# Output projection of eight tiles in four pairs by seven products of halves

## Chip, cores and metric

The kernel runs on one core of a Trainium2 chip. The metric is the device time of one execution in microseconds.

## Reference

Layer norm, sliding attention with dilation (32 heads of 20, window of 8 positions two apart), output projection, and a gate from a bilinear feed-forward layer.

```python
B, S, D, F = 1, 2048, 640, 1536
xn = layernorm(x)                              # no scale, no shift
q, k, v = heads(xn @ wqkv)                     # 32 heads of 20
logits = q . k[pos - 2 * (0..7)] * 20 ** -0.5  # positions below 0 masked
o = softmax(logits) @ v[pos - 2 * (0..7)]
s = o @ wo                                     # (2048, 640) @ (640, 640): the part changed
h = (xn @ w_gate) * (xn @ w_up)                # (2048, 1536)
out = x + s * silu(h @ w_down)
```

All is float32. A product is made of three: each operand is split into a high part (fp32r) and a low part, and high x high, high x low and low x high are summed (`mm3`, `ALL3`).

## The kernel before

The 2048 positions are 16 tiles of 128. The order on each engine is the order of the source; buffers are taken by tag (`st(shape, tag, bufs)`), and an operation waits until the buffer it takes is free. PSUM tags are q (4 banks), g (2) and u (2).

The stages follow each other and overlap. Norm and transposition of the tiles come first; then twelve units (`qkv`, `attention`) of q, k, v, whose attention runs on VectorE while TensorE works on pieces of gate and up (`gate_up(f, ch)`: block f of 12, 512 positions ch of 4). The last two blocks are f0 = 10 and f1 = 11; their eight pieces are written out by hand. In a piece, the first half of the matmuls fills a g bank, ScalarE copies it (`gs`, L409), the second half fills a u bank, and VectorE multiplies the two into `hs` (L420). This multiplication is issued a piece later (`finish_piece`), behind what the source puts on VectorE's queue between the pieces; the very last is made by ScalarE (L422) and GpSimd (L423). hs goes to `h_scr` in DRAM.

Then comes the output projection. `load_o` fetches attention rows of up to three tiles from `o_scr`, `trans_o` transposes a tile on VectorE (L481) and splits it (`split`, L85 on ScalarE for the high part, L86 for the low part), and `out_proj` makes two halves of 320 columns of 15 matmuls each: 5 blocks of the contraction x 3 parts. ScalarE copies each (L498); `s_scr` holds the results. The weights wo are loaded by `load_wo` and split by `split_wo` on ScalarE and GpSimd, five blocks k. Beside it, in twelve steps, the weights of the down projection are loaded (`load_wd`), summed on VectorE (`sum_wd`, L529 to L535) and split on ScalarE and GpSimd (`split_wd`).

Last, the down projection: pairs of tiles by seven products of halves in the Strassen-Winograd form (`product`, L620; `gather`; sums of h in `sum_h`, high and low parts in `hi_h`, `lo_h`), with silu, the gate and the result.

All DMAs are issued by the SP queue, in order. `load_h` fetches the pieces of h.

Of the kernel before, what the change touches and what calls it, by code (L numbers as in the profile page):

```python
# [11 lines left out]
F32 = mybir.dt.float32  # L12
F32R = mybir.dt.float32r
AF = mybir.ActivationFunctionType
# [5 lines left out]
P = 128  # L20
S, D, F = 2048, 640, 1536
# [16 lines left out]
SCALE = DH ** -0.5  # L38
MASKED = -1e9 / SCALE
EPS = 1e-5  # L40
PAIRS = range(0, W, 2)
PACE = 1.0

# [7 lines left out]
def kernel(  # L51
# [23 lines left out]
    def st(shape, tag, bufs, dt=F32):  # L75
        cnt[0] += 1
        return sb.tile(shape, dt, tag=tag, bufs=bufs, name=f"{tag}_{cnt[0]}")

    def pt(shape, tag, bufs):
        cnt[0] += 1  # L80
        return ps.tile(shape, F32, tag=tag, bufs=bufs, name=f"{tag}_{cnt[0]}")

    def split(eng, raw, hi, lo):

        nc.scalar.activation(hi, raw, AF.Copy)  # L85
        eng.tensor_sub(lo, raw, hi.bitcast(F32))  # L86
# [3 lines left out]
    def mm3(acc, pairs, parts=ALL3, first=True, last=True):  # L90

        pairs = list(pairs)
        runs = [(a[i], b[j]) for i, j in parts for a, b in pairs]
        for n, (a, b) in enumerate(runs):
            nc.tensor.matmul(acc, a, b, start=first and n == 0, stop=last and n == len(runs) - 1)  # L95
# [356 lines left out]
    def load_wo(ks):  # L452
        t = st([P, 2, D], "wraw", 3)
        for n, k in enumerate(ks):
            nc.sync.dma_start(t[:, n, :], wo[:, k, :])
            wo_raw[k] = t[:, n, :]
        return t

    def split_wo(k):
        if k < KD - 1:  # L460
            y = st([P, 2, D], ("wf", "wf", "wqh", "wql")[k], (4, 4, 1, 1)[k], F32R)
            hi, lo = y[:, 0], y[:, 1]
        else:
# [6 lines left out]
    def load_o(s, n, t):  # L470


        for b in range(NQ):
            nc.sync.dma_start(t[b * QB:(b + 1) * QB].rearrange("i n (q c) -> i (n q) c", c=QC),
                              o_scr[s // NE, b, s % NE:s % NE + n].rearrange("n (q i) c -> i (n q) c", i=QB))
        for i in range(n):
            o_t[s + i] = t[:, i]

    def trans_o(s):
        y = st([P, KD, P], "ot", 2)  # L480
        nc.vector.transpose(y.rearrange("p k (q i) -> p k q i", i=QB),  # L481
                            o_t.pop(s).rearrange("p (q k j) -> p k q j", q=NQ, j=QB))
        if s == NT - 2:
            oT[s] = st([P, KD, P], "hs", 2, F32R), st([P, KD, P], "hs", 2, F32R)
        else:
            tag, n = ("kv", 2) if s == 0 else ("wf", 4) if s < NT - 2 else ("t", 2)
            z = st([P, 2, KD, P], tag, n, F32R)
            oT[s] = z[:, 0], z[:, 1]
        split(nc.vector, y, *oT[s])

    def out_proj(s):
        a = oT.pop(s)
        y = st([P, D], "hs" if s % 2 and s < NT - 4 else "gs", 2)
        for n in range(2):
            c = slice(n * HALF, (n + 1) * HALF)
            p = pt([P, HALF], "q", 4)
            mm3(p, [([t[:, k, :] for t in a], [t[:, c] for t in wo_s[k]]) for k in range(KD)])
            nc.scalar.activation(y[:, c], p, AF.Copy)  # L498
        nc.sync.dma_start(s_scr[s], y)


    KH = KF // 2
# [1 line left out]
    W_IN = ("B11", "T1", "T2", "B22", "T3", "B21", "T4")  # L504
    H_IN = ("A11", "S1", "S2", "S4", "S3", "A12", "A22")

    def begin_wd():

        big = [st([P, KH + 2, 2, HALF], "xc", NCH, F32R) for _ in range(4)]
        for name, y in zip(("B11", "T1", "T2", "B21"), big):  # L510
            wd_t[name] = [y[:, k] for k in range(KH)]
        wd_t["T3"] = [big[k // 2][:, KH + k % 2] for k in range(KH)]
        for name in ("B22", "T4"):
            y = st([P, KH, 2, HALF], "kv", 2, F32R)
            wd_t[name] = [y[:, k] for k in range(KH)]

    def load_wd(k):
        wd_raw[k] = st([P, 2, 2, HALF], "wraw", 3)
        for a in range(2):
            nc.sync.dma_start(wd_raw[k][:, a].rearrange("p a c -> p (a c)"), wd[:, a * KH + k, :])  # L520
# [16 lines left out]
    def split_wd(k, part):  # L537
        for name in (("B11", "B22", "T1"), ("B21", "T2", "T3", "T4"))[part]:
            split(nc.gpsimd, wd_v[k][name], *(wd_t[name][k][:, i] for i in range(2)))
        if part:  # L540
            wd_raw.pop(k), wd_v.pop(k)

    h_raw, hT = {}, {}

    def load_h(n):

        a, b = 2 * n, 2 * n + 1
        if n % 2:
            ta, tb = st([P, KF, P], "t", 2), st([P, KF, P], "t", 2)
            nc.sync.dma_start(ta, h_scr[a])  # L550
            nc.sync.dma_start(tb, h_scr[b])
            h_raw[n] = {"A11": ta[:, :KH], "A12": ta[:, KH:], "A21": tb[:, :KH], "A22": tb[:, KH:]}
        else:
            h_raw[n] = {}
            for name, s, k, tag, m in (("A11", a, 0, "wraw", 3), ("A21", b, 0, "wraw", 3),
                                       ("A22", b, KH, "wraw", 3), ("A12", a, KH, "o", 1)):
                h_raw[n][name] = st([P, KH, P], tag, m)
                nc.sync.dma_start(h_raw[n][name], h_scr[s][:, k:k + KH])

# [63 lines left out]
    def gather(m):  # L623

        n, j = divmod(m, 7)
        a, b = 2 * n, 2 * n + 1
        p = bank["ACACABA"[j]]
        if j == 0:
            keep("M1", p, "lg", 2)
        elif j == 1:  # L630
            keep("M5", p, "lg", 2)
        elif j == 2:
            keep("U2", p, "e", 1)
        elif j == 3:
# [12 lines left out]
        return lambda: None  # L647


    begin_unit(0)  # L650
# [121 lines left out]
    for u in range(2, len(UN)):  # L772
        unit(u)
        for _ in range(3 + (u in (2, 5)) if u + 1 < len(UN) else len(pieces)):
            if len(pieces) == 1:
                load_wf(f1)
            piece()
    for ch in range(NCH):
        gate_up(f0, ch)
        if ch == 0:  # L780
            split_wf(f1, nc.gpsimd)
            load_wo((0, 1))
            load_wo((2, 3))
            t = load_wo((4,))
    for ch in range(NCH):
        if ch == 3:
            load_wd(0)
            trans_o(0)
            load_o(1, 1, st([P, 1, D], "o", 1))
            load_o(2, 3, st([P, 3, D], "t", 2))  # L790
            load_o(5, 3, st([P, 3, D], "t", 2))
        gate_up(f1, ch)
        if ch < 3:
            for k in ((0, 1), (2, 3), (4,))[ch]:
                split_wo(k)
        if ch == 1:
            drain(len(UN) - 2)
            load_o(0, 1, t[:, 1:2])
        if ch == 2:
            advance(1e9)  # L800

    load_wd(1)
    o_next = {3: (8, 3), 6: (11, 3), 9: (14, 2)}
    n_prod = 7 * NT // 2
    for s in range(NT):
        k, part = divmod(s - 1, 2)
        if s == 1:
            begin_wd()
        if s + 1 < NT:
            trans_o(s + 1)  # L810
        if s in o_next:
            load_o(*o_next[s], st([P, o_next[s][1], D], "t", 2))
        if 0 <= k < KH:
            sum_wd(k, part)
        out_proj(s)
        if 0 <= k < KH:
            split_wd(k, part)
            if part and k + 2 < KH:
                load_wd(k + 2)
        if s == 12:  # L820
            load_h(0)
        if s == 14:
            hi_h(0)
            lo_h(0)
# [72 lines left out]
```

## Time and profile before

| | |
|---|---|
| median of 3 runs | 782.94 us (782.87 to 783.04) |
| profiled execution | 783.04 us |
| its span, first to last instruction | 781.3 us |
| TensorE busy | 774.8 us, 4432 matmuls |
| VectorE busy | 670.1 us |
| ScalarE busy | 231.1 us |
| GpSimd busy | 135.8 us |

The span is what the profile shows of an execution; the rest of its time lies around it. Times of rows count from the span's start. PE is TensorE, PEld its weight loads, DVE VectorE, ACT ScalarE, POOL GpSimd, SPq the queue of the DMAs. L86 is line 86 of the kernel. `out<-in` names the program's tiles by tag; an idle time stands in brackets with what ended it.

### The profile page before, as it was taken

The numbers are of one execution on the slowest core, as the hardware profiler recorded it, in microseconds if no ns is written. First come the engines' busy times: TensorE is split into PE (matmuls) and PEld (weight loads), VectorE is DVE, ScalarE is ACT, GpSimd is POOL, SyncE is SP. The second block draws the span as 40 slices with busy tenths as digits, with TensorE's granted clock in tenths as the row PEclk, the third lists the DMA queues.
The fourth block names the chain that finished last, engine by engine and source line by source line (L and its number), as shares of the span: only waits on it lengthen the run. The fifth ranks groups of instructions, "written<-read, shape, count | busy, mean of one in ns | idle before, by whom it ended". The sixth has DMA issues, their size and how long they took to land.

```text
span 781.3 us, 11212 instructions
## 1 busy us (share of the span) xinstructions
PE 774.8 (99%) x4432; PEld 706.4 (90%) x4432; DVE 670.1 (86%) x694; ACT 231.1 (30%) x527; POOL 135.8 (17%) x109
## 2 busy tenths in 40 slices
PE   8999999999999999999999999999999999999997
PEld 7989898898988898989898989888899999999997
DVE  7999898999999999996999999995368677777775
ACT  4323312031112121312131212112256554444442
POOL 5200401021013101210204001023177600000000
PEclk9999999999999999999999999999999999999999
DMA  9562131331224122423133131432967574555534
GB/s 320 174 195 75 43 96 38 96 90 48 85 50 124 49 64 81 119 61 79 29 100 91 39 105 39 128 101 70 242 186 216 167 264 156 200 191 182 182 102 136
DMA packets 82237, 93.99 MB, mean 120 GB/s; under 512 B 23096, under 2 KB 63368, under 8 KB 82056
## 3 DMA queue, kind: packets, MB, share of 16 engines
q1 hardware_dynamic: 82184, 93.27, 39.2%
q8 instruction: 35, 0.57, 0.3%
q14 instruction: 18, 0.15, 0.1%
HBM read 55.84 MB, written 28.31 MB: 108 GB/s over the span
## 4 chain that ended last, share of the span: by engine, by line
PE 98%; DMA 0%; ACT 0%; SPq 0%; DVE 0%; issue 0%
PE q L306 27%; PE u L95 22%; PE g L95 22%; PE q L620 11%; PE q L95 9%; PE u L620 5%; PE g L620 3%; DMA wraw<-in_wqkv 0%; SPq L135 0%; ACT xc L231 0%; ACT wqh L85 0%; PE q L230 0%; DVE q L606 0%; DVE q L607 0%; ACT q L601 0%
## 5 line engine op out<-in xcount | busy, mean ns | idle before, releaser
L95 PE MATMUL u<-xc,wf 128*128 128x512 f32 (+1 forms) x735 | 176.2, 390 | 0.0
L95 PE MATMUL g<-xc,wf 128*128 128x512 f32 (+1 forms) x735 | 176.2, 390 | 0.0
L95 PEld LDWEIGHTS u<-xc,wf 128*128 128x128 f32 x735 | 135.7, 187 | 32.1
L95 PEld LDWEIGHTS g<-xc,wf 128*128 128x128 f32 x735 | 135.3, 188 | 31.0
L306 PE MATMUL q<-wqh,xc 128*128 128x300 f32 (+1 forms) x960 | 160.5, 310 | 0.3 <-ACT xc L231 0.2
L306 PEld LDWEIGHTS q<-wqh,xc 128*128 128x128 f32 x960 | 146.3, 188 | 2.7 <-ACT xc L231 0.8
L340 DVE TENSOR_TENSOR t<-q,kv 128x1600 f32<-128x1600 f32 (+1 forms) x48 | 96.9, 2019 | 8.2 <-ACT gs L409 7.2
L361 DVE TENSOR_TENSOR t<-e,kv 128x1600 f32<-128x1600 f32 (+1 forms) x48 | 97.6, 2049 | 1.1
L86 POOL TENSOR_TENSOR wf<-wraw,wf 128x256 fp32r<-128x256 f32 (+2 forms) x22 | 47.8, 2190 | 281.2 <-ACT wf L85 281.2
L343 DVE TENSOR_REDUCE lg<-t 128x80 f32<-128x1600 f32 (+1 forms) x48 | 92.6, 1929 | 1.1
L409 ACT ACTIVATE gs<-g 128x512 f32<-128x512 f32 x48 | 28.7, 598 | 213.8 <-PE g L95 208.6
L306 PE MATMUL q<-wql,xc 128*128 128x300 f32 (+1 forms) x480 | 86.2, 309 | 0.0
L369 DVE TENSOR_TENSOR t<-t,t 128x1600 f32<-128x1600 f32 (+1 forms) x36 | 75.2, 2089 | 1.0
L308 ACT ACTIVATE kv<-q 128x200 f32<-128x200 f32 (+1 forms) x96 | 33.4, 348 | 143.3 <-PE q L306 143.1
L306 PEld LDWEIGHTS q<-wql,xc 128*128 128x128 f32 x480 | 74.8, 188 | 0.0
L620 PE MATMUL q<-xc,wf 128*128 128x320 f32 x432 | 67.2, 308 | 0.0
L620 PEld LDWEIGHTS q<-xc,wf 128*128 128x128 f32 x432 | 64.3, 188 | 0.0
L86 POOL TENSOR_TENSOR wql<-wraw,wqh 128x300 fp32r<-128x300 f32 (+4 forms) x14 | 33.2, 2394 | 168.1 <-ACT wqh L85 168.0
L420 DVE TENSOR_TENSOR hs<-u,gs 128x512 f32<-128x512 f32 x47 | 32.1, 682 | 10.4 <-PE u L95 9.5
L95 PE MATMUL q<-wf,wf 128*128 128x320 f32 x156 | 35.1, 305 | 0.0
L86 DVE TENSOR_TENSOR wf<-ot,wf 128x640 fp32r<-128x640 f32 x13 | 15.0, 1157 | 21.0 <-ACT wf L85 18.1
L95 PEld LDWEIGHTS q<-wf,wf 128*128 128x128 f32 x156 | 26.0, 188 | 0.0
(172 smaller groups left out, 883.4 us busy)
## 6 DMA issues: line engine op xcount, KB each, us to landing
h_scr<-hs SPq DMA_DIRECT2D x48, 256.0 KB, 2.4
wraw<-in_wgu SPq DMA_DIRECT2D x12, 640.0 KB, 4.7
t<-h_scr SPq DMA_DIRECT2D x8, 768.0 KB, 7.7
hs<-s_scr SPq DMA_DIRECT2D x16, 320.0 KB, 3.6
gs<-in_x SPq DMA_DIRECT2D x16, 320.0 KB, 4.2
wraw<-h_scr SPq DMA_DIRECT2D x12, 384.0 KB, 6.3
out<-q SPq DMA_DIRECT2D x14, 320.0 KB, 2.6
wraw<-in_wd SPq DMA_DIRECT2D x12, 320.0 KB, 3.9
```

Of the source, the lines that this page charges most:

```text
L86: eng.tensor_sub(lo, raw, hi.bitcast(F32))
L95: nc.tensor.matmul(acc, a, b, start=first and n == 0, stop=last and n == len(runs) - 1)
L306: nc.tensor.matmul(p, xT[(r * NE + i) // TPC][a][:, k, t0:t0 + P], wq[g][b][:, k], start=n == 0, stop=n == len(runs) - 1, skip_group_check ...
L308: nc.scalar.activation(kv_t[u][:, :, W - 1 + i, :], p[:, c:].rearrange("p (a c) -> p a c", a=2), AF.Copy)
L340: nc.vector.tensor_mul(t, q.rearrange("p i c -> p (i c)").unsqueeze(1).to_broadcast([P, 2, NE * c]), places(0, j))
L343: nc.vector.tensor_reduce(out=lg[:, :, j:j + 2].rearrange("p n a -> p a n"), in_=heads(t), op=ALU.add, axis=AX.X)
L361: nc.vector.tensor_mul(heads(t), pw, heads(places(1, j)))
L369: nc.vector.tensor_add(acc, acc, t)
L409: nc.scalar.activation(gs, pp[0], AF.Copy)
L420: nc.vector.tensor_mul(hs, pp[1], gs)
L620: nc.tensor.matmul(p, y[:, i, k], wd_t[name][k][:, l], start=new and r == 0, stop=r == len(runs) - 1, skip_group_check=True)
```

## The change

Tiles 0 to 7 are projected as four pairs. The pair's rows are a 2 x 2 matrix of blocks (two tiles by two halves of two contraction blocks each), wo's first four blocks are another (two by two halves of 320 columns), and seven products of halves give the four results, in the order and banks of the down projection. The fifth contraction block is added directly: three matmuls in each of products 3 to 6, in product 6 with the difference of its two column halves. The sums of wo (`sums_wo`, `sum_w5`) are made in place in its raw buffers and split by ScalarE and GpSimd (`split_t`, `split_w5`); the sums of a pair are made by VectorE (`turn_pair`), the high parts by ScalarE (`hi_pair`), the low parts by VectorE (`lo_pair`). These operands lie in pieces of buffers that the down projection's weights take later (`blocks`). Pair 0 is loaded after piece (f0, 2) into the buffer of k and v that is free by then.

Blocks 2 and 3 of wo are split after pieces (f0, 1) and (f0, 2) instead of after (f1, 1); the sums and splits of wo and the first pairs stand between the pieces of f1. The twelve steps of the down weights run to tile 14 instead of tile 12, two of them together in pair 3. `load_h(0)` is issued in two parts, and A21 goes to another buffer. Tiles 8 to 15 are projected as before.

```diff
-    def trans_o(s):
-        y = st([P, KD, P], "ot", 2)
+    def turn(y, s):
         nc.vector.transpose(y.rearrange("p k (q i) -> p k q i", i=QB),
                             o_t.pop(s).rearrange("p (q k j) -> p k q j", q=NQ, j=QB))
...
+    def blocks(y, r, h, n):
+        return y[:, r:].rearrange("p r i c -> p (r i c)")[:, :h * n * P].rearrange("p (h n c) -> p h n c", h=h, c=P)
...
+    def sums_wo():
+        r, u = wo_keep
+        b11, b12, b21, b22 = r[:, :, :HALF], r[:, :, HALF:], u[:, :, :HALF], u[:, :, HALF:]
+        nc.vector.tensor_sub(b11, b12, b11)
+        nc.vector.tensor_sub(b12, b22, b12)
+        nc.vector.tensor_sub(b22, b22, b11)
+        nc.vector.tensor_sub(b21, b21, b22)
+        wo_keep.append({"T1": b11, "T3": b12, "T2": b22, "T4": b21})
+
+    def sum_w5():
+        w = wo_keep[3]
+        nc.vector.tensor_sub(w[:, :HALF], w[:, :HALF], w[:, HALF:])
+
+    def split_t(name, y, r):
+        v = wo_keep[2][name]
+        t = y[:, r:r + KS]
+        split(nc.gpsimd, v, t[:, :, 0], t[:, :, 1])
...
+    def turn_pair(p):
+        y = pair_y[p] = st([P, 2, KD, P], "ot", 2)
+        for i in range(2):
+            turn(y[:, i], 2 * p + i)
+        s1, s2, s4 = (pair_raw[p][:, i * KS:(i + 1) * KS] for i in range(3))
+        a11, a12, a21, a22 = (y[:, i, k:k + KS] for i in range(2) for k in (0, KS))
+        nc.vector.tensor_add(s1, a21, a22)
+        nc.vector.tensor_sub(s2, s1, a11)
+        nc.vector.tensor_sub(s4, a12, s2)
+        nc.vector.tensor_sub(a21, a11, a21)
...
+    def hi_pair(p, part):
...
+        nc.scalar.activation(z[0], raw, AF.Copy)
+
+    def lo_pair(p, part):
+        z, raw = pair_z[p, part]
+        nc.vector.tensor_sub(z[1], raw, z[0].bitcast(F32))
...
+    FIFTH = {3: ("a5", HALF), 4: ("b5", HALF), 5: ("a5", 0), 6: ("b5", None)}
+
+    def pair_product(p, j):
+        place = "ACACABA"[j]
+        new = j in (0, 1, 5)
...
+        runs = [(pair_in(p, H_IN[j], k, i), w_part(W_IN[j], k, l)) for i, l in ALL3 for k in range(KS)]
+        if j in FIFTH:
+            name, c = FIFTH[j]
+            runs += [(pair_in(p, name, 0, i), wo_t["W0-W1"][:, l] if c is None else wo_s[KD - 1][l][:, c:c + HALF])
+                     for i, l in ALL3]
+        for r, (y, w) in enumerate(runs):
+            nc.tensor.matmul(b, y, w, start=new and r == 0, stop=r == len(runs) - 1, skip_group_check=True)
+        kept, (ya, yb) = pair_k[0], y_t.setdefault((p, "y"), [None, None])
+        if j < 3:
+            nc.scalar.activation(kept[:, j], b, AF.Copy)
...
     for ch in range(NCH):
         gate_up(f0, ch)
         if ch == 0:
             split_wf(f1, nc.gpsimd)
...
+        elif ch < 3:
+            split_wo(ch + 1)
+        if ch == 2:
             drain(len(UN) - 2)
+            load_pair(0)
+    gate_up(f1, 0)
+    advance(1e9)
+    split_wo(0)
+    split_wo(1)
+    load_pair(1)
+    load_pair(2)
+    begin_wd("T4")
+    begin_wd()
+    turn_pair(0)
+    gate_up(f1, 1)
+    split_wo(4)
+    for i in range(3):
+        hi_pair(0, i)
+    sums_wo()
+    wo_keep.append(w5)
+    split_t("T1", wd_big[0], 4)
+    split_t("T2", wd_big[0], 6)
+    sum_w5()
+    split_w5()
+    for i in range(3):
+        lo_pair(0, i)
+    begin_wd()
+    turn_pair(1)
+    gate_up(f1, 2)
+    split_t("T3", wd_big[1], 4)
+    split_t("T4", wd_big[1], 6)
+    load_wd(0)
     load_wd(1)
+    begin_wd()
+    turn_pair(2)
+    gate_up(f1, 3)
+    begin_wd()
+    begin_wd("B22")
+    sum_wd(0, 0)
...
+    pair_product(0, 0)
+    for p in range(SP // 2):
+        more = p + 1 < SP // 2
+        n = (1, 0, 1, 2)[p]
+        if not more:
+            y8 = turn_o(SP)
+        wd_sums(n)
+        pair_product(p, 1)
+        if more:
+            hi_pair(p + 1, 0)
+            lo_pair(p + 1, 0)
+        else:
+            split_o(SP, y8)
+        pair_product(p, 2)
+        if more:
+            hi_pair(p + 1, 2)
+        pair_product(p, 3)
+        if more:
+            lo_pair(p + 1, 2)
+            hi_pair(p + 1, 1)
+        if p == 0:
+            split_wd(0, 0)
+        pair_product(p, 4)
+        wd_splits(n)
+        if more:
+            lo_pair(p + 1, 1)
+        pair_product(p, 5)
+        if p == 0:
+            load_pair(3)
+        elif p == 1:
+            load_o(SP, 3, st([P, 3, D], "t", 2))
+            turn_pair(3)
+        elif p == 2:
+            load_o(SP + 3, 3, st([P, 3, D], "t", 2))
+        if more:
+            pair_product(p + 1, 0)
+        else:
+            out_proj(SP, 0)
+        pair_product(p, 6)
...
+            load_h(0, ("A11", "A21", "A12"))
+        elif s == 13:
+            load_h(0, ("A22",))
```

More of the change, by code (lines that the diff above doesn't have):

```diff
@@ L40 @@
 EPS = 1e-5
+SP = NT // 2
 PAIRS = range(0, W, 2)
@@ L477, in load_o, with turn_o, trans_o, split_o @@
             o_t[s + i] = t[:, i]
-    def trans_o(s):
-        y = st([P, KD, P], "ot", 2)
+    def turn(y, s):
         nc.vector.transpose(y.rearrange("p k (q i) -> p k q i", i=QB),
                             o_t.pop(s).rearrange("p (q k j) -> p k q j", q=NQ, j=QB))
+    one_t = []
+    def turn_o(s):
+        if not one_t:
+            one_t.append(st([P, 2, KD, P], "ot", 2))
+        y = one_t[0][:, s % 2]
+        turn(y, s)
+        return y
+    def trans_o(s):
+        split_o(s, turn_o(s))
+    def split_o(s, y):
         if s == NT - 2:
@@ L485, in trans_o, with out_proj @@
         else:
-            tag, n = ("kv", 2) if s == 0 else ("wf", 4) if s < NT - 2 else ("t", 2)
-            z = st([P, 2, KD, P], tag, n, F32R)
+            if s == SP:
+                z = blocks(wd_kv["B22"], 4, 2, KD)
+            else:
+                z = st([P, 2, KD, P], *(("wf", 4) if s < NT - 2 else ("t", 2)), F32R)
             oT[s] = z[:, 0], z[:, 1]
         split(nc.vector, y, *oT[s])
[L491 to L499, printed above, removed]
+    y_t = {}
+    def out_proj(s, n):
+        a = oT[s]
+        if n == 0:
+            y_t[s] = st([P, D], "hs" if s % 2 and s < NT - 4 else "gs", 2)
+        c = slice(n * HALF, (n + 1) * HALF)
+        p = pt([P, HALF], "q", 4)
+        mm3(p, [([t[:, k, :] for t in a], [t[:, c] for t in wo_s[k]]) for k in range(KD)])
+        nc.scalar.activation(y_t[s][:, c], p, AF.Copy)
+        if n:
+            oT.pop(s)
+            nc.sync.dma_start(s_scr[s], y_t.pop(s))
     KH = KF // 2
@@ L505, with begin_wd @@
     H_IN = ("A11", "S1", "S2", "S4", "S3", "A12", "A22")
[L507 to L515, printed above, removed]
+    wd_big, wd_kv = [], {}
+    def begin_wd(kv=None):
+        if kv:
+            y = wd_kv[kv] = st([P, KH, 2, HALF], "kv", 2, F32R)
+            wd_t[kv] = [y[:, k] for k in range(KH)]
+            return
+        y = st([P, KH + 2, 2, HALF], "xc", NCH, F32R)
+        wd_t[("B11", "T1", "T2", "B21")[len(wd_big)]] = [y[:, k] for k in range(KH)]
+        wd_big.append(y)
+        if len(wd_big) == NCH:
+            wd_t["T3"] = [wd_big[b][:, k] for b, k in ((2, 6), (2, 7), (3, 7), (3, 6), (1, 6), (1, 7))]
+    def blocks(y, r, h, n):
+        return y[:, r:].rearrange("p r i c -> p (r i c)")[:, :h * n * P].rearrange("p (h n c) -> p h n c", h=h, c=P)
     def load_wd(k):
@@ L543, with load_h @@
     h_raw, hT = {}, {}
-    def load_h(n):
+    def load_h(n, names=()):
         a, b = 2 * n, 2 * n + 1
@@ L553, in load_h @@
         else:
-            h_raw[n] = {}
-            for name, s, k, tag, m in (("A11", a, 0, "wraw", 3), ("A21", b, 0, "wraw", 3),
-                                       ("A22", b, KH, "wraw", 3), ("A12", a, KH, "o", 1)):
+            h_raw.setdefault(n, {})
+            for name, s, k, tag, m in (("A11", a, 0, "wraw", 3), ("A21", b, 0, *(("wraw", 3) if n else ("ot", 2))),
+                                       ("A12", a, KH, "o", 1), ("A22", b, KH, "wraw", 3)):
+                if names and name not in names:
+                    continue
                 h_raw[n][name] = st([P, KH, P], tag, m)
@@ L647, in gather @@
         return lambda: None
+    KS = KD // 2
+    wo_t = {}
+    def sums_wo():
[9 more added lines that the diff above has]
+        nc.vector.tensor_sub(w[:, :HALF], w[:, :HALF], w[:, HALF:])
@@ new lines, in split_t, with split_w5, w_part @@
+    def split_t(name, y, r):
+        v = wo_keep[2][name]
+        t = y[:, r:r + KS]
+        split(nc.gpsimd, v, t[:, :, 0], t[:, :, 1])
+        wo_t[name] = [t[:, k] for k in range(KS)]
+    def split_w5():
+        t = wd_kv["T4"][:, KH - 1]
+        split(nc.gpsimd, wo_keep[3][:, :HALF], t[:, 0], t[:, 1])
+        wo_t["W0-W1"] = t
+    def w_part(name, k, l):
+        if name in wo_t:
+            return wo_t[name][k][:, l]
+        a, c = divmod(int(name[1:]) - 11, 10)
+        return wo_s[a * KS + k][l][:, c * HALF:(c + 1) * HALF]
@@ new lines, with load_pair @@
+    pair_raw, pair_y, pair_z, pair_k = {}, {}, {}, []
+    def load_pair(p):
+        if p:
+            t = st([P, 3, D], "t", 2)
+            load_o(2 * p, 2, t[:, 0:2])
+            t = t.rearrange("p a c -> p (a c)")
+        else:
+            t = st([P, 2, D], "kv", 2)
+            load_o(0, 2, t)
+            t = t.rearrange("p a c -> p (a c)")
+        pair_raw[p] = t[:, :3 * KS * P].rearrange("p (a c) -> p a c", c=P)
+    def turn_pair(p):
[8 more added lines that the diff above has]
+        nc.vector.tensor_sub(a21, a11, a21)
@@ new lines, in hi_pair @@
+    def hi_pair(p, part):
+        if part == 2:
+            if p % 2:
+                z = [st([P, 2, KD, P], "wf", 4, F32R).rearrange("p a k c -> p (a k) c")[:, :3 * KS] for _ in range(2)]
+            else:
+                z = blocks(wd_kv["T4"], 2, 2, 3 * KS) if p else blocks(wd_big[0], 1, 2, 3 * KS)
+                z = [z[:, 0], z[:, 1]]
+            raw = pair_raw[p]
+        else:
+            y, r = (wd_big[3], 3) if p % 2 else (wd_kv["B22"], 2) if p else (wd_kv["T4"], 1)
+            z = blocks(y, r, 2, 2 * KD)
+            z = [z[:, i, part * KD:(part + 1) * KD] for i in range(2)]
+            raw = pair_y[p][:, part]
+        pair_z[p, part] = z, raw
+        nc.scalar.activation(z[0], raw, AF.Copy)
@@ new lines, in lo_pair, with pair_in @@
+    def lo_pair(p, part):
+        z, raw = pair_z[p, part]
+        nc.vector.tensor_sub(z[1], raw, z[0].bitcast(F32))
+    def pair_in(p, name, k, i):
+        part, b = {"A11": (0, 0), "A12": (0, KS), "a5": (0, 2 * KS), "S3": (1, 0), "A22": (1, KS), "b5": (1, 2 * KS),
+                   "S1": (2, 0), "S2": (2, KS), "S4": (2, 2 * KS)}[name]
+        return pair_z[p, part][0][i][:, b + k]
+    FIFTH = {3: ("a5", HALF), 4: ("b5", HALF), 5: ("a5", 0), 6: ("b5", None)}
+    def pair_product(p, j):
+        place = "ACACABA"[j]
+        new = j in (0, 1, 5)
+        if new:
+            bank[p, place] = pt([P, HALF], {"A": "q", "B": "g", "C": "u"}[place], {"A": 4, "B": 2, "C": 2}[place])
+        b = bank[p, place]
+        runs = [(pair_in(p, H_IN[j], k, i), w_part(W_IN[j], k, l)) for i, l in ALL3 for k in range(KS)]
[8 more added lines that the diff above has]
+            nc.scalar.activation(kept[:, j], b, AF.Copy)
+        elif j == 3:
+            ya = y_t[p, "y"][0] = st([P, D], "gs", 2)
+            nc.vector.tensor_add(ya[:, HALF:], kept[:, 2], b)
+        elif j == 4:
+            yb = y_t[p, "y"][1] = st([P, D], "hs", 2)
+            nc.vector.tensor_add(yb[:, HALF:], kept[:, 1], b)
+        elif j == 5:
+            nc.vector.tensor_add(ya[:, :HALF], kept[:, 0], b)
+            nc.sync.dma_start(s_scr[2 * p], ya)
+        else:
+            nc.scalar.activation(yb[:, :HALF], b, AF.Copy)
+            nc.sync.dma_start(s_scr[2 * p + 1], yb)
@@ L777 @@
             piece()
+    wo_keep = []
     for ch in range(NCH):
@@ L781, with wd_sums, wd_splits @@
             split_wf(f1, nc.gpsimd)
[L782 to L796, printed above, removed]
-            drain(len(UN) - 2)
-            load_o(0, 1, t[:, 1:2])
-        if ch == 2:
-            advance(1e9)
-    load_wd(1)
[L803 to L813, printed above, removed]
+            wo_keep += [load_wo((0, 1)), load_wo((2, 3))]
+            w5 = load_wo((4,))[:, 0]
+        elif ch < 3:
+            split_wo(ch + 1)
+        if ch == 2:
+            drain(len(UN) - 2)
+            load_pair(0)
[26 more added lines that the diff above has]
+    load_wd(0)
+    load_wd(1)
+    begin_wd()
[4 more added lines that the diff above has]
+    sum_wd(0, 0)
+    pair_k.append(st([P, 3, HALF], "o", 1))
+    wd_steps = [(k, part) for k in range(KH) for part in range(2)][1:]
+    def wd_sums(n):
+        for k, part in wd_steps[:n]:
             sum_wd(k, part)
-        out_proj(s)
-        if 0 <= k < KH:
+    def wd_splits(n):
+        for k, part in wd_steps[:n]:
             split_wd(k, part)
@@ L819 @@
                 load_wd(k + 2)
+        del wd_steps[:n]
+    pair_product(0, 0)
[9 more added lines that the diff above has]
+            lo_pair(p + 1, 0)
+        else:
+            split_o(SP, y8)
[22 more added lines that the diff above has]
+            pair_product(p + 1, 0)
+        else:
+            out_proj(SP, 0)
+        pair_product(p, 6)
+    n_prod = 7 * NT // 2
+    for s in range(SP, NT):
+        if s + 1 < NT:
+            trans_o(s + 1)
+        if s == SP + 2:
+            load_o(SP + 6, 2, st([P, 2, D], "t", 2))
+        wd_sums(1)
+        if s > SP:
+            out_proj(s, 0)
+        out_proj(s, 1)
+        wd_splits(1)
         if s == 12:
-            load_h(0)
+            load_h(0, ("A11", "A21", "A12"))
+        elif s == 13:
+            load_h(0, ("A22",))
         if s == 14:
```

## The prediction

> **What bounds the kernel now.** I read the parts of the page first: busy time, the chain that ended last, then TensorE's list of waits.
>
> ```profile
> span 781.3 us, 11212 instructions
> PE 774.8 (99%) x4432; PEld 706.4 (90%) x4432; DVE 670.1 (86%) x694; ACT 231.1 (30%) x527; POOL 135.8 (17%) x109
> PE 98%; DMA 0%; ACT 0%; SPq 0%; DVE 0%; issue 0%
> PE q L157 <- POOL ident masks.py:199: 1.4, 1, 1.4
> PE q L230 <- issue: 0.3, 1, 0.3
> PE q L306 <- ACT xc L231: 0.2, 1, 0.2
> ```
>
> The first two lines are the span and the busy times, the third the chain by engine, the last three TensorE's whole list of waits (total, times, longest): 1.9 us, all at the start. TensorE's stream is the time. A matmul taken out counts in full, and so does every wait put in, unless another engine's cover holds. So I price the matmuls, then look for the engine whose cover is thin. A difference under 0.2% (1.6 us: 781.4 to 784.5 about the median 782.94) is about what a measurement here can't tell from none.
>
> **The matmuls.** The pitch of the projection comes from ScalarE's copies of its results (start, us, what): the first half tile and the last, 31 halves apart. The pitch of products by halves comes from the windows view of the down projection (stretch, its us, PE busy and count, PEld, DVE, ACT, POOL).
>
> ```profile
> 561.50 0.44 ACT L498 ACTIVATE gs<-q 128x320 f32<-128x320 f32 x1 [1.03 <-PE q L95]
> 629.14 0.44 ACT L498 ACTIVATE gs<-q 128x320 f32<-128x320 f32 x1 [1.74 <-PE q L95]
> 629.00:781.00 152.00, 147.90 (x1009) 147.64 (x1007) 115.71 (x147) 67.81 (x113) 0.00 (x0) 1.00 0.51 179
> ```
>
> 67.64 / 31 = 2.182 us for 15 matmuls, 0.1455 each. A pair of tiles costs 60 now. After, it costs 7 products x 2 blocks x 3 parts = 42, and the fifth block of the contraction adds 3 to each of four products: 54. Eight tiles: 240 x 0.1455 = 34.9 us become 216. In the down projection a matmul of the same 320 columns takes 147.90 / 1008 = 0.1467 us; at this pitch 216 take 31.7, at the other 31.4. The gain is **3.2 to 3.5 us**. I take 3.2, since the second row's form is the one the change uses.
>
> **What VectorE and GpSimd get to do while gate and up still run.** Their covers decide, so here is that stretch (start, us, engine, line, what, idle before).
>
> ```profile
> 534.14 1.16 DVE L372 TENSOR_TENSOR o<-t 128x960 f32<-128x960 f32 x1
> 538.30 0.69 DVE L420 TENSOR_TENSOR hs<-u,gs 128x512 f32<-128x512 f32 x1 [3.00 <-PE u L95]
> 545.30 0.69 DVE L420 TENSOR_TENSOR hs<-u,gs 128x512 f32<-128x512 f32 x1 [6.31 <-PE u L95]
> 545.90 0.83 DVE L481 STREAM_TRANSPOSE ot<-wraw 128x640 f32<-128x640 f32 x1
> 550.63 1.67 DVE L86 TENSOR_TENSOR kv<-ot,kv 128x640 fp32r<-128x640 f32 x1 [3.89 <-ACT kv L85]
> 552.24 0.69 DVE L420 TENSOR_TENSOR hs<-u,gs 128x512 f32<-128x512 f32 x1
> 536.04 3.09 POOL L86 TENSOR_TENSOR wf<-wraw,wf 128x640 fp32r<-128x640 f32 x2 [22.92 <-ACT wf L85]
> 544.56 1.58 POOL L86 TENSOR_TENSOR wql<-wraw,wql 128x640 fp32r<-128x640 f32 x1
> 550.04 1.57 POOL L86 TENSOR_TENSOR q<-wraw,q 128x640 fp32r<-128x640 f32 x1 [3.90 <-ACT q L85]
> ```
>
> The attention ends at 535.3. A piece of gate and up takes 7.0 us (538.30 to 545.30). VectorE multiplies each piece's u out of its bank (L420) as soon as the piece ends, and idles between.
>
> Two operations with both inputs in SBUF exclude each other: at 550.63 VectorE's subtraction takes 1.67 us beside GpSimd's that began at 550.04, and ends 0.69 after it. Alone the same form takes 0.83:
>
> ```profile
> 580.46 0.83 DVE L86 TENSOR_TENSOR wf<-ot,wf 128x640 fp32r<-128x640 f32 x1 [0.87 <-ACT wf L85]
> 581.20 0.48 DVE L534 TENSOR_TENSOR wraw<-wraw 128x320 f32<-128x320 f32 x1
> 583.71 1.50 DVE L86 TENSOR_TENSOR wf<-ot,wf 128x640 fp32r<-128x640 f32 x1 [0.87 <-ACT wf L85]
> 585.13 1.16 DVE L529 TENSOR_TENSOR lg<-wraw 128x320 f32<-128x320 f32 x1
> 584.49 1.46 POOL L86 TENSOR_TENSOR kv<-e,kv 128x320 fp32r<-128x320 f32 x1
> ```
>
> GpSimd's 584.49 waits in turn for VectorE's end at 585.21, and L529 for GpSimd's end at 585.95: they take turns. The multiplication out of a bank (0.69 at 545.30, under GpSimd's 544.56) and the transposition (0.83 at 545.90) aren't delayed. The Trainium skill ("SBUF — State Buffer", Who interferes with whom) says the same and speaks against this change: GpSimd shares a port pair with VectorE as an exclusive lock, and a tensor_tensor with both inputs in SBUF contends. Were that not so, only the sum without lock, below, would hold.
>
> Into this stretch the change puts, in VectorE's order: two transpositions and four sums of 256 columns (turn_pair 0), the multiplication of piece (f1, 0), four sums of 640 (sums_wo), one of 320, three low parts (640, 640, 768), turn_pair(1), and only then the multiplication of piece (f1, 1). By start-to-start times (0.74 for 640 at 580.46; 0.41 for 320; by the same slope 0.34 for 256 and 0.87 for 768; 0.1 more where an operation reads the one before), a turn_pair is 3.25, sums_wo 3.2, the low parts 2.4, with sum_w5 0.4 and two multiplications 1.3: 13.8 us. **Without lock**, from 535.3, that ends at 549.1. On GpSimd stand eight splits: blocks 0, 1, 4, then T1, T2, W0-W1, T3, T4, 1.5 us each, one 0.8.
>
> When must it be done? The u banks are two: piece (f1, 3) writes (f1, 1)'s, from the middle of the piece on.
>
> ```profile
> 516.48 0.56 DVE L356 TENSOR_TENSOR e<-e,sm 128x384 f32<-128x384 f32 x1
> 521.93 2.16 DVE L369 TENSOR_TENSOR t<-t,t 128x1920 f32<-128x1920 f32 x1
> 524.30 0.69 DVE L420 TENSOR_TENSOR hs<-u,gs 128x512 f32<-128x512 f32 x1 [0.21 <-PE u L95]
> 514.85 0.53 ACT L352 ACTIVATE e<-lg 128x384 f32<-128x384 f32 x1 [0.51 <-DVE lg L350]
> 520.80 0.60 ACT L409 ACTIVATE gs<-g 128x512 f32<-128x512 f32 x1 [5.43 <-PE g L95]
> 541.74 0.60 ACT L409 ACTIVATE gs<-g 128x512 f32<-128x512 f32 x1 [5.15 <-PE g L95]
> 555.80 0.60 ACT L409 ACTIVATE gs<-g 128x512 f32<-128x512 f32 x1 [5.21 <-PE g L95]
> 559.24 0.60 ACT L422 ACTIVATE hs<-u 128x512 f32<-128x512 f32 x1 [2.83 <-PE u L95]
> ```
>
> The copy at 555.80 follows the end of that piece's first half by some 0.3 us, so the deadline is about 555.5.
>
> **With lock.** Blocks 2 and 3 of the output weights are now split during the attention. ScalarE can start the first at 515.3 behind the exponential; GpSimd holds 516.0 to 517.6, so L356 (516.48) loses 1.05 us. The second follows the copy at 520.80: GpSimd asks at 522.0 and gets in ahead of L369, another 1.4, less the 0.2 idle before 524.30. Block 0, due at 536.04, gets in ahead of the last sum: the attention ends at 538.7. Then, turn by turn: block 1 to 540.1 beside the transpositions, sums to 541.9, multiplication to 542.5, T1's sum 543.2, block 4 (its copy behind 541.74) 544.6, T3's 545.3, T2's 546.05, T1's split 547.5, T4's sum 548.2, T2's split 549.6, sum_w5 549.9, low part 550.7, W0-W1 551.4, low part 552.1, T3's split 553.5, low part 554.3, turn_pair(1) 557.5 beside T4's split, multiplication 558.15. TensorE waits from 555.5 to 558.2: **2.7 us**. Bounds: 0 by the sum without lock; 4.1 if T4's split gets a turn of its own too. I take 2.7, since every subtraction of 640 at L86 shown beside GpSimd took 1.50 or 1.67.
>
> **The rest of the change.** TensorE restarts at 558.2, the first product at 561.7. The second product needs (f1, 2)'s u bank at 562.6: turn_pair(2) and its multiplication end at 562.0, since GpSimd is idle then. The queue of the DMAs (SP) is in order: wd's first two loads stand behind (f1, 1)'s store, 558.2, hence 559.
>
> ```profile
> wraw<-in_wd SPq DMA_DIRECT2D x12, 320.0 KB, 3.9
> L343 DVE TENSOR_REDUCE lg<-t 128x80 f32<-128x1600 f32 (+1 forms) x48 | 92.6, 1929 | 1.1
> ```
>
> By the first row (issue to landing) they land at about 563.3. sum_wd(0, 0) waits for that at the head of VectorE's queue, with lo_pair(1, 0) and the additions of pair 0 behind it; eight steps later, 567.6, the addition that product 6 needs at 569.2 is done. Nothing, but thin. (The second row is the reduction: one input, no lock; it costs the attention nothing.)
>
> Within a pair (7.9 us) VectorE has at most 7.5 us of work, ScalarE 6, both paced by TensorE. A copy of a product is 0.44 and the bank's next product is one product (0.88) away: covered by 0.1 to 0.2. In pair 3 two down-weight steps are summed ahead of the split of the first: the second T2 needs the buffer that GpSimd's split of the first T2 frees, while lo of tile 8 and two additions queue behind it on VectorE. Copy of product 2, two ScalarE splits, two on GpSimd: 29.3 us into the pairs; the additions end at 32.8, product 6 wants them at 32.6. I take **0.3 us** (0 to 1.3: every one of three subtractions locked out for 0.7, less what is spare).
>
> load_pair(0) goes to SP four transfers early, with unit 10's stores long done; pairs 1 and 2 follow the attention's store and have over 10 us. The last weight step now falls in tile 14: ScalarE starts hi_h(0) 1.5 us later, and tile 15's 4.4 us cover it. A22's load, a tile later, is needed a tile and a half on. Those cost nothing; with tile 15's cover gone they'd cost at most 1.5.
>
> **Sum.** The profiled execution took 783.04, 1.7 around its span of 781.3 and 0.1 over the median. 783.04 - 3.2 + 2.7 + 0.3 = 782.8; less the 0.1 to the median, **782.7**.
>
> **Rivals.** *The cover holds* (0.36): VectorE was idle 13 us between 535.3 and 550.6 (3.00, 6.31 and 3.89 in the rows), and if GpSimd's splits fall beside transpositions, or the attention isn't delayed, the multiplication ends by 556.5 and the wait is under 1. Then 783.04 - 3.2 (or 3.5) + 0 to 1 + 0 to 0.3: 779.5 to 781.1, say 780.3. Against: VectorE has no slack before 535, and eight splits meet it. *wd lands late* (0.17): should the two loads take 6 us, sum_wd(0, 0) starts 2.3 us later, and past a landing at 564.8 the addition for product 6 of pair 0 is late: 0.8 us, and another 1.1 from the splits that then meet those subtractions. 784.6; slower. For it: loads queue beside pair loads and h stores; against: 3.9 was their median.
>
> *The clock falls* (0.05): in the trace the granted clock is 1.00 in each stretch shown, with no idle over 1.4 us. If a wait of over 3 us halves it, the half piece behind the wait, 3.5 us, takes 7.0: 786.3. The Trainium skill ("TensorE: Matmul & The Clock Gate", Why this matters for your kernels) asks for no idle gaps over about 3 us; no run here shows one.
>
> **The numbers.** The forecast's own case, waits of 1.5 to 4.1, has 0.42, within 781.1 to 784.2. From the four cases: faster 0.37, same 0.41, slower 0.22. Range 779.7 to 784.9: the lower end nearly all of the first rival, the upper one with late wd, without the clock.
>
> **What would show it.** Right: TensorE waits once for VectorE's L420 in piece (f1, 3), 1.5 to 4 us; L420 of (f1, 1) starts past 556; L86 and the new sums take 1.2 to 1.7 beside GpSimd; the pairs take 31.4 to 31.7 of TensorE's time plus under 1 of waits. Wrong: no wait there (then 780), or waits at the first pair's products, or matmuls of the pairs with another pitch.

## The result and the profile after

The changed kernel takes 785.4 us (median of 7 runs, 783.59 to 785.88), the kernel before 782.97 on the same chip: a ratio of 1.0026, with a 95% interval of 1.0014 to 1.0038. It is slower by 2.4 us, though TensorE has 24 matmuls less. The seven runs are two groups: 783.59 and 784.05, called the first group below, and five from 785.37 to 785.88, the later group. The profile shown first is of the fastest run.

The page of the changed kernel: span, busy times, chain by engine.

```profile
span 781.7 us, 11227 instructions
PE 771.9 (99%) x4408; PEld 702.7 (90%) x4408; DVE 694.9 (89%) x731; ACT 236.6 (30%) x536; POOL 147.4 (19%) x114
...
PE 91%; DVE 5%; issue 1%; DMA 1%; SPq 1%; ACT 0%; DVEq 0%
```

The head of its TensorE's list of waits (who for whom: total, times, longest):

```profile
PE u L96 <- DVE hs L421: 2.6, 1, 2.6
```

The chain that ended last now runs through VectorE for 5% of the span, and one new wait of 2.6 us stands at the head of the list: the u half of piece (f1, 3), for the multiplication that frees its bank. The timeline of VectorE and GpSimd ahead of it (start, us, engine, line, what):

```profile
516.49 1.58 DVE L357 TENSOR_TENSOR e<-e,sm 128x384 f32<-128x384 f32 x1
...
522.96 3.40 DVE L370 TENSOR_TENSOR t<-t,t 128x1920 f32<-128x1920 f32 x1
...
536.12 2.52 DVE L373 TENSOR_TENSOR o<-t 128x960 f32<-128x960 f32 x1
...
542.35 0.81 DVE L688 TENSOR_TENSOR wraw<-wraw 128x640 f32<-128x640 f32 x1
543.20 2.12 DVE L689 TENSOR_TENSOR wraw<-wraw,wraw 128x640 f32<-128x640 f32 x1
545.35 0.83 DVE L690 TENSOR_TENSOR wraw<-wraw,wraw 128x640 f32<-128x640 f32 x1
546.21 2.08 DVE L691 TENSOR_TENSOR wraw<-wraw 128x640 f32<-128x640 f32 x1
548.21 1.85 DVE L696 TENSOR_TENSOR wraw<-wraw 128x320 f32<-128x320 f32 x1
549.99 2.24 DVE L758 TENSOR_TENSOR kv<-ot,kv 128x640 fp32r<-128x640 f32 x2
552.15 2.32 DVE L758 TENSOR_TENSOR xc<-kv,xc 128x768 fp32r<-128x768 f32 x1
554.39 1.55 DVE L481 STREAM_TRANSPOSE ot<-t 128x640 f32<-128x640 f32 x2
...
557.58 0.68 DVE L421 TENSOR_TENSOR hs<-u,gs 128x512 f32<-128x512 f32 x1
...
516.09 1.56 POOL L87 TENSOR_TENSOR wqh<-wraw,wqh 128x640 fp32r<-128x640 f32 x1 [2.95 <-ACT wqh L86]
522.12 2.23 POOL L87 TENSOR_TENSOR wql<-wraw,wql 128x640 fp32r<-128x640 f32 x1 [4.47 <-ACT wql L86]
536.05 4.02 POOL L87 TENSOR_TENSOR wf<-wraw,wf 128x640 fp32r<-128x640 f32 x2 [11.70 <-ACT wf L86]
543.05 1.57 POOL L87 TENSOR_TENSOR q<-wraw,q 128x640 fp32r<-128x640 f32 x1 [2.98 <-ACT q L86]
545.67 4.04 POOL L87 TENSOR_TENSOR xc<-wraw,xc 128x640 fp32r<-128x640 f32 x2 [1.04 <-ACT xc L86]
```

Three attention operations lose 1.0 to 1.4 us each (0.56, 2.16 and 1.16 before), each beside a split of wo on GpSimd (516.09, 522.12 and 536.05); of the four sums of 640 two take 2.1 us instead of 0.8, and the one of 320 takes 1.85, each until GpSimd has had its turn. The multiplication of (f1, 1) ends at 558.26; the bank was wanted at 555.7.

### The profile page after: what moved, and what is told of

The parts are those of the page before. It is cut to its first block, busy times and chain, and to the rows that moved or that the text cites. A ratio compares the mean times of both kernels' runs of the same rounds, so it can differ in the third digit from the quotient of the medians.

```text
span 781.7 us, 11227 instructions
## 1 busy us (share of the span) xinstructions
PE 771.9 (99%) x4408; PEld 702.7 (90%) x4408; DVE 694.9 (89%) x731; ACT 236.6 (30%) x536; POOL 147.4 (19%) x114
## 4 chain that ended last, share of the span: by engine, by line
PE 91%; DVE 5%; issue 1%; DMA 1%; SPq 1%; ACT 0%; DVEq 0%
PE q L307 27%; PE u L96 19%; PE g L96 18%; PE q L650 10%; PE u L650 5%; PE q L96 4%; PE g L650 3%; PE q L779 2%; PE u L779 1%; DVE t L370 1%; PE g L779 1%; DMA t<-o_scr 1%; DMA wraw<-in_wqkv 1%; DVE t L362 1%; SPq L475 1%
## 5 line engine op out<-in xcount | busy, mean ns | idle before, releaser
L87 POOL TENSOR_TENSOR xc<-wraw,xc 128x320 fp32r<-128x320 f32 (+1 forms) x22 | 26.4, 1204 | 25.1 <-ACT xc L86 24.6
L310 ACT ACTIVATE q<-q 128x100 f32<-128x100 f32 (+1 forms) x96 | 24.6, 256 | 0.0
L613 DVE TENSOR_TENSOR wf<-t,wf 128x768 fp32r<-128x768 f32 x16 | 15.3, 957 | 8.5 <-ACT wf L609 7.8
```

## The experiments

**The changed kernel again (again).** The groups of times had no explanation in the first profile.

> The changed kernel once more, unchanged. Its seven runs fell into two groups, 783.6 to 784.1 and 785.4 to 785.9; the profile at hand is of the first. Theory A (a TensorE wait of 2.7 us in piece (f1, 3) lets the clock fall for a few microseconds, depending on where the wait falls in the clock's own period): again two groups some 2 us apart, and a profile of the later group shows matmuls at twice the pitch behind that wait. Theory B (something else that differs between executions, such as a late DMA and a second wait): a profile of the later group shows another wait of about 2 us and no doubled pitch.

785.33 us, 1.0023 of before (1.0014 to 1.0032). Of the ten runs two take 783.77 and 783.83 and eight from 785.17 to 785.54. The profile fell into the later group, as Theory A has it. The windows view around the wait (stretch, its us, PE busy, PEld, DVE, ACT, POOL, granted clock, DMA share, GB/s), first of this run:

```profile
548.69:555.69 7.00, 7.00 (x31) 5.45 (x29) 7.00 (x6) 2.21 (x4) 5.86 (x4) 1.00 0.01 2
555.69:558.69 3.00, 0.37 (x2) 0.20 (x2) 2.90 (x7) 0.14 (x1) 0.38 (x1) 1.00 0.00 0
558.69:562.10 3.41, 3.41 (x9) 2.64 (x9) 3.31 (x7) 0.46 (x1) 0.00 (x0) 0.50 0.79 208
562.10:569.10 7.00, 7.00 (x45) 6.62 (x44) 3.90 (x8) 4.47 (x10) 1.90 (x2) 1.00 0.73 231
```

and the same stretch of the first profile, of the first group:

```profile
558.69:562.10 3.41, 3.41 (x17) 2.78 (x16) 3.31 (x8) 0.29 (x1) 0.00 (x0) 1.00 0.84 252
```

Behind the same wait (2.6 us in both) the clock is granted at a half for 3.41 us: 9 matmuls where the other run has 17, 1.7 us lost. The spans differ by as much (783.4 and 781.7).

**TensorE kept at work during the wait.**

> Four products of the identity (0.64 us each by the start of the trace, 2.6 us together) put between the two halves of piece (f1, 3), so that TensorE works while it waits for the bank; nothing else is changed. Theory A (idle clock): one group of times only, 783.6 within 0.5, as the first group of the changed kernel. Theory B: two groups as before, 783.6 and 785.8. If the products delay the second half themselves, all times rise by under 0.3.

```diff
-    gate_up(f1, 3)
+    gate_up(f1, 3, amid=[lambda: idle_product(3)] * 4)
```

783.91 us (783.56 to 784.69, 11 runs), 1.0007 of before (0.9998 to 1.0015). Three runs lie above the 784.1 that was expected at most, but none reaches the later group. TensorE's and VectorE's timelines:

```profile
556.64 2.75 PE L158 MATMUL q<-ident 128*128 128x384 f32 x8
```

```profile
558.70 0.68 DVE L421 TENSOR_TENSOR hs<-u,gs 128x512 f32<-128x512 f32 x1
```

The multiplication is as late as ever, but TensorE's list of waits has no line for it. The idle is the cause of the half clock, since nothing else was taken away. Executions some 1 to 2 us longer than the rest come without this wait too: of 66 runs of the kernel before, taken beside these kernels, 7 lie 0.8 to 1.8 us above their median, and no profile shows why. So one or two of the 13 in the later group may have another cause.

**The two turns moved behind the multiplication (later_turns).**

> turn_pair(1) moved behind piece (f1, 2) and turn_pair(2) behind product 5 of pair 0, so that the multiplication of (f1, 1) stands right behind the low parts, at about 554.4, ahead of the deadline at 555.5. My theory (the wait is the place of turn_pair(1) in VectorE's queue, ahead of the multiplication): no wait in (f1, 3), 2.6 us less than the first group, 780.9 to 781.4, and one group of times. Rival (VectorE is late by its whole work, and whatever moves away comes back as a wait at the first pairs' products): 783 or more, with waits for lo_pair or the additions in pairs 0 and 1.

```diff
-    turn_pair(1)
     gate_up(f1, 2)
+    turn_pair(1)
...
-    turn_pair(2)
     gate_up(f1, 3)
...
         if p == 0:
+            turn_pair(2)
             load_pair(3)
```

780.97 us (780.59 to 781.22, 6 runs), 0.9968 of before (0.9956 to 0.998); in a second set of runs:

> later_turns once more, for the comparison on the same chip: 780.6 to 781.3, one group, no wait in (f1, 3).

781.11 us (780.79 to 781.51, 7 runs), 0.9972 (0.9961 to 0.9983). Both medians are as expected; one group each. The timeline of VectorE has the multiplication at 554.48, ahead of the transpositions:

```profile
554.48 0.68 DVE L421 TENSOR_TENSOR hs<-u,gs 128x512 f32<-128x512 f32 x1
555.08 1.55 DVE L481 STREAM_TRANSPOSE ot<-t 128x640 f32<-128x640 f32 x2
```

and TensorE's list of waits has no line for it. The wait was turn_pair(1)'s place in the queue; turn_pair(2) stood behind this multiplication before as well (558.18 in the first profile). This version takes less time than both kernels, by 0.3% against before.

**The low parts of the sums of wo made by VectorE.** This tells the lock from the amount of work.

> The low parts of T1 to T4 and W0-W1 made by VectorE instead of GpSimd: VectorE gets 3.4 us more work of its own. Theory of the lock (VectorE is late because it waits for GpSimd's turns): the multiplication of (f1, 1) starts at about 554.7 instead of 557.6 and TensorE's wait is under 0.3 us; 780.9 to 781.4. Rival (VectorE is late because of the amount of its work): the multiplication starts later than 557.6, the wait grows to 4 to 6 us, 785 to 789.

```diff
-        split(nc.gpsimd, v, t[:, :, 0], t[:, :, 1])
+        split(nc.vector, v, t[:, :, 0], t[:, :, 1])
...
-        split(nc.gpsimd, wo_keep[3][:, :HALF], t[:, 0], t[:, 1])
+        split(nc.vector, wo_keep[3][:, :HALF], t[:, 0], t[:, 1])
```

781.94 us (781.39 to 783.81, 10 runs), 0.9981 (0.9972 to 0.999). The timeline of VectorE, then the wait:

```profile
546.69 0.82 DVE L691 TENSOR_TENSOR wraw<-wraw 128x640 f32<-128x640 f32 x1
547.44 1.55 DVE L87 TENSOR_TENSOR xc<-wraw,xc 128x640 fp32r<-128x640 f32 x2
...
549.93 0.49 DVE L87 TENSOR_TENSOR kv<-wraw,kv 128x320 fp32r<-128x320 f32 x1 [0.54 <-ACT kv L86]
550.34 1.55 DVE L758 TENSOR_TENSOR kv<-ot,kv 128x640 fp32r<-128x640 f32 x2
551.81 0.95 DVE L758 TENSOR_TENSOR xc<-kv,xc 128x768 fp32r<-128x768 f32 x1
...
555.88 0.68 DVE L421 TENSOR_TENSOR hs<-u,gs 128x512 f32<-128x512 f32 x1
```

```profile
PE u L96 <- DVE hs L421: 0.4, 1, 0.4
```

The same subtractions take 0.82 (L691) and 0.95 (768 columns) where they took 2.08 and 2.32, and with more work of its own ahead of it the multiplication starts 1.7 us sooner. It wasn't the 2.9 expected (554.7): 0.4 of wait is left where under 0.3 was expected, VectorE stands 0.5 us for ScalarE's high part of W0-W1, and the time is above the 780.9 to 781.4 expected. The lock is the larger cost; the work isn't nothing.

**Blocks 2 and 3 of wo split late.**

> The changed kernel with blocks 2 and 3 of wo split behind blocks 0 and 1, after piece (f1, 0), so that no split meets the attention. My sum has the attention delayed by 2.2 us through the two early splits and by 1.2 through block 0. If that delay is passed on to the multiplication of (f1, 1): the wait shrinks from 2.6 to about 0.5, 781.5. If the turns only move (the two splits then meet turn_pair(0)'s sums and hold back sums_wo): attention ends near 535.3, sums_wo starts no earlier than 542.3, the wait is 2.6 to 4.2 and the time 784 to 788.

```diff
-        elif ch < 3:
-            split_wo(ch + 1)
...
-    split_wo(0)
-    split_wo(1)
+    for k in range(4):
+        split_wo(k)
```

786.76 us (786.48 to 787.19, 4 runs), 1.0044 (1.0029 to 1.0058). The timeline of VectorE, the wait, and the windows view right behind it:

```profile
534.47 1.16 DVE L373 TENSOR_TENSOR o<-t 128x960 f32<-128x960 f32 x1
...
538.27 1.67 DVE L735 TENSOR_TENSOR kv<-kv,ot 128x256 f32<-128x256 f32 x1
539.98 1.68 DVE L736 TENSOR_TENSOR kv<-ot,kv 128x256 f32<-128x256 f32 x1
...
558.90 0.68 DVE L421 TENSOR_TENSOR hs<-u,gs 128x512 f32<-128x512 f32 x1
```

```profile
PE u L96 <- DVE hs L421: 3.6, 1, 3.6
```

```profile
560.56:563.97 3.41, 3.41 (x10) 2.63 (x9) 2.97 (x7) 0.00 (x0) 0.00 (x0) 0.50 1.00 299
```

The attention ends 3 us sooner (535.6, not 538.6), and more than all of it is lost again: the small sums of turn_pair(0) now meet the splits (1.67 and 1.68 in these rows, 0.42 in the first profile), the multiplication starts 1.3 us later, the wait is 3.6, and the clock falls. The turns only move, as the second case had it.

**Shorter and longer waits.** Spare transpositions ahead of the multiplication in later_turns, two and seven (the edit shows two).

> later_turns with two spare transpositions (0.74 us each start to start; their result is not used) ahead of the multiplication of (f1, 1) on VectorE, which then ends at about 556.6: TensorE waits 1.0 to 1.2 us in (f1, 3). Theory A (the clock falls when TensorE idles most of one 3.4 us period): 1.1 over later_turns, 782.1, one group, no half clock in the profile. Rival (any wait at this place can lose the clock): some executions another 1.7 higher.

> The same with seven spare transpositions: the multiplication ends at about 560.3 and TensorE waits some 4.8 us, longer than the 3.4 us for which the clock was halved in the profile of again. Theory A: every execution loses the clock, 781.0 + 4.8 + 1.7 = 787.5 in one group (0.5 less or more where part of the half clock falls into the wait itself). Rival (the clock falls by chance, whatever the length): two groups again, 785.8 and 787.5.

```diff
+    spare = st([P, KD, P], "ot", 2)
+    for _ in range(2):
+        nc.vector.transpose(spare.rearrange("p k (q i) -> p k q i", i=QB),
+                            pair_y[0][:, 0].rearrange("p k c -> p (k c)").rearrange("p (q k j) -> p k q j", q=NQ, j=QB))
     gate_up(f1, 2)
     turn_pair(1)
```

With two, the wait is 1.0 and the time 782.28 (781.98 to 782.9, 10 runs; 0.9985, 0.9976 to 0.9995): one group, no half clock in the profile. With seven, the wait and the windows view behind it:

```profile
PE u L96 <- DVE hs L421: 5.4, 1, 5.4
```

```profile
560.83:564.24 3.41, 3.17 (x8) 2.49 (x9) 3.31 (x8) 0.60 (x1) 0.00 (x0) 0.50 0.65 174
```

5.4 instead of 4.8, and 788.48 (787.76 to 789.32, 4 runs; 1.0065, 1.005 to 1.008): 7.4 over later_turns, the wait and a half clock in each run as far as the times tell. The size missed by 1.0, of which 0.6 is the longer wait.

**The weight steps.** Two small waits were left in later_turns, before tile 8's low part and at product 2 of the down projection.

> later_turns with the weight steps 1, 0, 2, 2 in the pairs instead of 1, 0, 1, 2: the second T2 of pair 3 finds its buffer free, and the last step falls in tile 13. Theory (the 0.3 us before tile 8's low part and the 0.4 us at product 2 of the down projection come from these two places): 780.3, 0.6 to 0.7 under later_turns. Rival (the two steps crowd pair 2): the same or slower, 781.0 to 781.8, with a wait for L788 in pair 2.

```diff
-        n = (1, 0, 1, 2)[p]
+        n = (1, 0, 2, 2)[p]
```

782.08 us (781.82 to 783.6, 10 runs; 0.9987, 0.9978 to 0.9996), 1.1 over later_turns and a little above the rival's 781.8. It is the rival's mechanism: both small waits are gone, but there is a new one (TensorE's waits, then VectorE's timeline):

```profile
PE q L779 <- DVE hs L788: 1.2, 1, 1.2
```

```profile
582.77 1.23 DVE L758 TENSOR_TENSOR wf<-t,wf 128x768 fp32r<-128x768 f32 x1
583.92 0.47 DVE L788 TENSOR_TENSOR hs<-o,q 128x320 f32<-128x320 f32 x1
```

The addition for product 6 of pair 2 is late behind the second step.

> later_turns with one weight step in pair 3 and two each in tiles 8 and 9 (steps 1, 0, 1, 1 in the pairs), so that pair 2 stays as it was, pair 3 sums no T2 ahead of the split that frees its buffer, and the last step falls in tile 13. Theory (the 0.3 us before tile 8's low part is the T2 buffer, the 0.4 us at product 2 of the down projection is GpSimd's last split beside the sum S1): neither wait is left, 0.6 under later_turns. Rival (two steps crowd tiles 8 and 9 as they crowded pair 2): a wait for a low part in tiles 9 to 11, no gain or a loss up to 1.

```diff
-        n = (1, 0, 1, 2)[p]
+        n = (1, 0, 1, 1)[p]
...
-        wd_sums(1)
+        n = 2 if s < SP + 2 else 1
+        wd_sums(n)
...
-        wd_splits(1)
+        wd_splits(n)
```

785.93 us (785.6 to 786.49, 5 runs; 1.0035, 1.0023 to 1.0048), 4.8 over later_turns. Neither case had it: again both small waits are gone, but the loss is far over the rival's 1, and the waits go on past its tiles 9 to 11. The larger waits are for ScalarE's high parts of tiles 11 to 14, behind splits that wait for VectorE's sums, which wait for GpSimd. TensorE's largest wait, then the timeline of VectorE and that of ScalarE:

```profile
PE q L96 <- ACT wf L86: 3.7, 3, 2.5
```

```profile
603.84 1.15 DVE L563 TENSOR_TENSOR e<-wraw,lg 128x320 f32<-128x320 f32 x1
...
605.02 0.47 ACT L86 ACTIVATE kv<-e 128x320 fp32r<-128x320 f32 x1 [0.60 <-DVE e L563]
605.83 0.74 ACT L86 ACTIVATE wf<-ot 128x640 fp32r<-128x640 f32 x1 [0.35 <-DVE ot L481]
```

So the places of the two small waits are shown. That one step to a tile is about what these stages carry is argued from these two runs.

## Why the prediction was wrong

Forecast 782.7 in a range of 779.7 to 784.9; measured 785.4.

- *The matmuls.* Right: 4408 instead of 4432, and the pairs' pitch is the down projection's (both 0.147 us a matmul in the first profile). From the first product of the output projection (561.92) to the first of the down projection (629.03) it takes 67.1 us, where it took 69.9 before (559.04 to 628.94): 2.8 less, against 2.9 predicted (3.2 less 0.3).
- *The wait in piece (f1, 3).* Right, and to its steps: attention's end 538.6 (538.7 predicted), multiplication's end 558.26 (558.15), wait 2.6 (2.7). Turning the pairs later shows the place, the low parts on VectorE the lock. The sign of 1.2 to 1.7 us for a sum beside GpSimd was too low: those rows have 1.85 to 2.12. The Trainium skill ("SBUF — State Buffer", Who interferes with whom) has GpSimd share a port pair with VectorE as an exclusive lock. The rows agree: sums of 640 take 0.8 where they start ahead of a split and 2.1 where they start behind one, the multiplication out of a bank 0.68 throughout.
- *The clock.* The step that failed: the sum puts nothing for the clock behind its own wait of 2.7 us. A fall stood only as a rival with a chance of 0.05, on the condition of a wait of over 3 us, for 3.5 us. It took no more than the wait that came, 2.6: of 17 runs of this kernel 13 are in the later group, and the profile of one of them shows the half clock and 1.7 us lost by it. I had the wait right and let its length decide, where its place in the clock's period decides.
- *How the period shows.* The records of the granted clock show full clock for 552.959 us and then half for 3.413 in again: 162 times 3.413, so the stretches come in one period; the stretches at full clock in the other traces are whole multiples of it too (64 to 228 times). Carried back from where the clock changes, the period's borders fall as follows; idle is counted here from one pitch (0.23 us) behind the start of the last matmul, which makes 2.8 of the 2.6 in the list of waits. In again the last full period, 555.3 to 558.7, holds all of the idle (2.8 of 3.4 us); in the first profile the border fell at 557.5 and left 1.9 and 0.8 us on either side, and the clock stayed. The late split of wo left 2.5 in one period, and it fell. In the profile with two weight steps each in tiles 8 and 9 a border parted a wait of 2.5 by the list into 1.8 and 0.9, and the clock stayed. So by these four profiles the border lies between 1.9 and 2.5 us of idle in one period of 3.4. The Trainium skill ("TensorE: Matmul & The Clock Gate", What's actually happening) has this free-running window of 3413 ns, and the period above agrees. The Trainium skill's advice against gaps of over about 3 us ("TensorE: Matmul & The Clock Gate", Why this matters for your kernels), on which I set the condition, is too generous for this case: 2.6 us was enough, and the measurement decides.
- *The size of a fallen clock.* Wrong by half: I doubled the whole half piece; the half clock lasts one period, and 3.41 us of it cost 1.7. The rival's price for the clock was 1.8 too high.
- *Pair 3.* Right: 0.3 before tile 8's low part, for the T2 buffer; VectorE sat idle 3.6 us at that sum (first profile of the changed kernel):

```profile
591.38 1.14 DVE L558 TENSOR_TENSOR lg<-wraw,lg 128x320 f32<-128x320 f32 x1 [3.63 <-POOL xc L87]
```

- *The last weight step in tile 14.* Mis-sized at nothing. I covered ScalarE's delay, which is covered, and forgot the lock: GpSimd's last split meets the sum S1 on VectorE (their timeline in the same profile, then S1 before):

```profile
628.94 1.62 DVE L597 TENSOR_TENSOR wqh<-ot,wraw 128x768 f32<-128x768 f32 x1
...
628.17 1.58 POOL L87 TENSOR_TENSOR kv<-e,kv 128x320 fp32r<-128x320 f32 x1
```

```profile
628.85 0.96 DVE L567 TENSOR_TENSOR wqh<-wraw,wraw 128x768 f32<-128x768 f32 x1 [1.99 <-PE q L95]
```

S1 takes 1.62 instead of 0.96, and the down projection is 0.35 late from product 2 on. Both kernels that end the steps a tile sooner don't have this wait.

- *wd lands late* didn't happen: L558's wait for it was 0.7 us, long ahead of product 6.

For the first profile the steps give 782.8 against 783.59: 0.2 more until the first product, 0.35 in the down projection, 0.1 each in the pairs and around the span. The other 1.8 of the median is the clock, 1.7 of it seen in the profile of again.

The range failed by leaving the fallen clock out. An estimate of its chance, from these profiles: if the wait falls at any place in the period alike, 2.8 us of idle puts at least 1.9 us into one period in 0.7 of the executions, and at least 2.5 in 0.35. 13 of 17 are nearer the first. The forecast with a fallen clock would have been 782.7 + 1.7 = 784.4.

## What to carry to other kernels

A saving on the bounding engine is worth what the operands' preparation leaves of it: list the queue of the engine that frees the banks, in order, with every operation of the engine that shares its port, and put what has a deadline ahead of what has none (here two lines moved, 4.4 us). On TensorE, a wait is priced at its length plus the clock it may lose: here nothing more was lost at 1.0 us, mostly another 1.7 at 2.6, and spare products in the gap avoided that.

## What the runs showed of the hardware

Behind a single idle of 2.6 us in over 500 us of full work the granted clock fell to 0.50 for one period of 3.41 us in one profile of the changed kernel, and stayed at 1.00 in the other, where the period's border parted the idle. By the times it fell in 13 of 17 executions, so one program has two times, 1.7 us apart. Idle of 1.0 us left the clock at 1.00 in its profile, and none of its ten times shows a fall. Where the border lies between 1.9 and 2.5 us of idle in one period wasn't tried.

Where VectorE and GpSimd both subtract from SBUF to SBUF they take turns: 640 columns take VectorE 0.82 us alone and up to 2.12 beside GpSimd's split of 1.57, while a transposition and a multiplication out of a bank keep their times.
